# A second buffer for the split halves of v ahead of their DMA transpose

## The chip, the cores and the metric

The kernel runs on one core of a Trainium2 chip. The metric is the device time of one execution in microseconds (us), the median of several runs. The engines are TensorE (PE in the profile, with PEld for its weight loads), VectorE (DVE), ScalarE (ACT), GpSimd (POOL) and SyncE (SP), which here only issues DMAs. Each engine works through its own instructions in a fixed order; semaphores hold an instruction back until what it depends on is done.

## The reference

Causal attention with a bias from a running sum, for 8 batches of 8 heads, 576 positions and 64 channels, and then a feed-forward layer on its result:

```python
scores = scale * np.matmul(q, k.transpose(0, 1, 3, 2))
s_pos = np.maximum(s, 0.0)
cum = np.cumsum(s_pos, axis=-1)
bias = -(cum[:, :, :, None] - cum[:, :, None, :])
scores = np.where(causal, -1000000000.0, scores + np.minimum(bias, 0.0))
attn = softmax(scores)                       # with 1e-09 added to the sum
x = np.matmul(attn, v)                       # heads side by side: (4608, 512)
h = x @ w_in                                 # (4608, 2048)
g = np.where(h >= 1, h, np.where(h <= -1, 0.0, (h + 1) ** 2 / 4))
out = g @ w_out                              # (4608, 512)
```

All inputs and the output are float32.

## The kernel before

Most products are made of 16-bit parts: a float32 value is scaled and split into a high half and a low half (the remainder), and three of the four products of halves are summed. So `WI`, `WO`, `x`, `g`, `pb` and `vb` all have two halves.

**Jobs and slots.** The attention is cut into 64 jobs: for each batch, four pairs of heads for the first half of the positions (`hf` 0, positions 0 to 319) and then the same four pairs for the second half (`hf` 1). `att_slot(j, k)` traces slot k (0 to 7) of job j. Slot 0 prepares the operands of the scores (`att_prep`: `Q1s`, `K1s`, `Q2s`, `K2s`, lines 353 to 363), slot 1 of an `hf` 0 job prepares v (`v_prep`), slots 2 to 7 make the scores of one tile each, slot 5 of an `hf` 0 job turns v (`v_turn`), and slot 7 multiplies the weights of the job before with its v (`att_out`, line 474, into `px`). The feed-forward steps (`ffn_h`, line 528, and `ffn_y`, line 567) of an earlier half batch are traced between the slots. During the first two batches the weights `w_in` and `w_out` are also decoded and split on DVE, ACT and POOL.

**The way of v.** For each pair of heads n, counted through all batches (n = 4b + p), v lies in a float32 tile of 128 by 576 (`vraw`, loaded by line 256 on SP). `batch_v` (lines 260 to 265) works out the scales `rc` of a batch. `v_prep` opens the tile `vb` (128 by 2 by 640, float16): POOL zeroes its padding (line 371) and writes the high half, v times scale (line 372). For the first four tiles POOL makes the low half too (lines 374 and 375); for all others DVE does it in `v_turn` (line 382), queued behind a given step of the scores. Then line 384 has SP issue a DMA that transposes `vb` into `vt`, which `att_out` reads. `vt` has five buffers, `vb` one.

**The weights' way.** In `scores`, line 403 (POOL) zeroes an edge of the tile `p`, lines 408 to 412 (PE) make the scores `s`, line 417 (DVE) adds the mask and takes the minimum, line 428 (ACT) takes the exponential. `weights_t` then scales and splits the result into `pb`: `rs` (lines 444 and 445, DVE), high halves (lines 449 and 451, POOL), a scaling (line 450, ACT), low halves (line 452 POOL, line 455 DVE), and line 456 has SP issue the DMA transpose of `pb` into `pt`. In the feed-forward part, `u` comes from lines 540 to 544 (ACT, DVE), the high half of `g` from line 554 (ACT), the low half from line 555 (POOL).

**What sets the order.** The order of instructions on each engine isn't the order of the code. The program is built in a tile context with `schedule_with_timeline_sim=True`: when it is built, a simulated timeline runs along, and each engine is given, at each point of that timeline, an instruction whose inputs are ready and whose tile has a free buffer; among several the earlier in the code goes first, apart from blocks marked `high_priority` (a lead) and `issue_after` (behind a given instruction). A tile's buffer is free again when all its readers and writers are done: for `vb`, when the DMA transpose has landed. On the chip the order is fixed, and an instruction whose buffer isn't free yet holds up all that stands behind it on its engine.

Of the kernel before, what the change touches and what calls it, by code (L numbers as in the profile page):

```python
# [8 lines left out]
F16 = mybir.dt.float16  # L9
# [13 lines left out]
P = 128  # L23
# [4 lines left out]
SP = NB * P  # L28
# [45 lines left out]
def attention_ffn(ctx: ExitStack, tc: tile.TileContext, qT, kT, vT, s, w_in, w_out, yT):  # L74
# [5 lines left out]
    ap = ctx.enter_context(tc.tile_pool(name="ap", bufs=2))  # L80
# [284 lines left out]
    def v_prep(n):  # L365

        b, p = n // NPAIR, n % NPAIR
        v = vraw.pop((b, p))
        r = rcs[b][:, p:p + 1]
        VB = ap.tile([P, 2, SP], F16, tag="vb", bufs=1, name=f"vb{n}")  # L370
        G.memset(VB[:, :, S:], 0.0)
        G.tensor_scalar(VB[:, 0, :S], v, r, 1.0, ALU.mult, ALU.mult)
        if n < V_POOL:
            G.tensor_scalar(v, v, r, 1.0, ALU.mult, ALU.mult)
            G.tensor_tensor(VB[:, 1, :S], v, VB[:, 0, :S], ALU.subtract)
        vbs[n] = VB, v, r

    def v_turn(n):
        VB, v, r = vbs.pop(n)
        if n >= V_POOL:  # L380
            with tc.issue_after(ttr[0]):
                V.scalar_tensor_tensor(VB[:, 1, :S], v, r, VB[:, 0, :S], ALU.mult, ALU.subtract)
        VT = vts[n] = ap.tile([P, 2 * NB, P], F16, tag="vt", bufs=5, name=f"vt{n}")
        nc.sync.dma_start_transpose(out=VT, in_=VB.rearrange("p l n -> p (l n)"))
# [109 lines left out]
    def att_slot(j, k):  # L494

        if j < len(jobs):
            n, hf = jobs[j]
            if k == 0:
                att_prep(n, hf)
            if k == 1 and hf == 0:  # L500
                v_prep(n)
            if k == V_K and hf == 0:
                v_turn(n)
            if k >= 2:
                scores(n, *UNITS[hf][k - 2])
            if k == 3 and j + 1 < len(jobs):
                att_load(*jobs[j + 1])
            if k == 1 and j % (2 * NPAIR) == V_J and j // (2 * NPAIR) + 1 < B:
                load_v(j // (2 * NPAIR) + 1)
            if k == 5 and j + 1 < len(jobs) and jobs[j + 1][0] % NPAIR == 0 and jobs[j + 1][1] == 0:  # L510
                with tc.issue_after(ttr[0]):
                    batch_start(jobs[j + 1][0] // NPAIR)
        if k == OUT_K and 1 <= j <= len(jobs) and j != NPAIR:
            while j == len(jobs) and late:
                late.pop(0)()
            att_out(*jobs[j - 1])
# [171 lines left out]
```

## Time and profile before

| | us |
|---|---|
| median of 3 runs | 1111.91 |
| lowest and highest | 1111.22, 1112.82 |
| the profiled execution | 1112.3 |
| span of its instructions | 1110.2 |

The mean granted clock of TensorE over the span is 0.982 of full speed. The first 200 us are the start: weights are loaded, decoded and split there, and PE is far from full. From then on the slices of the span show PE at 9 tenths or more almost throughout. The page gives the busy time of each engine, 40 slices of the span, the DMA queues, the chain of work that ended last, and the costliest groups of instructions by line. The list of waits tells which engine stood still at which line, and what released it; the timeline has single instructions in order of time.

### The profile page before, as it was taken

Reading aid. Unit: us, or ns where it says so; the run is one execution under the profiler, and the core shown is the slowest. Engines: PE = TensorE matmul, PEld = TensorE weight load, DVE = VectorE, ACT = ScalarE, POOL = GpSimd, SP = SyncE. Lnnn points to the kernel's source line nnn. Section 1 sums busy time; section 2 is a strip of 40 time slices with the busy share of each in tenths; the row PEclk is TensorE's granted clock in tenths of the full one; section 3 lists DMA queues with packets and bytes.
Section 4 is the critical chain, followed back from the end, with each engine's and each line's share of the span. In section 5 each row is a group of like instructions: output and inputs, shape, how many; then the busy total and the mean of one; then the engine's idle time right before and its main releaser. Section 6 shows DMA issues by size and latency. Waiting matters only on the chain.

```text
span 1110.2 us, 25043 instructions
## 1 busy us (share of the span) xinstructions
PE 999.0 (90%) x8470; PEld 771.2 (69%) x8470; DVE 855.0 (77%) x2392; ACT 715.9 (64%) x1683; POOL 657.2 (59%) x1161
## 2 busy tenths in 40 slices
PE   0454799899999999999999999999999999899998
PEld 0132466588767877777777877787777877787787
DVE  7979987578868877878787877787777886887533
ACT  3647766467557775777567775877576755777432
POOL 3666275676647664766566755766476665765522
PEclk9997899699999999999999999999999999999999
DMA  8984536767638763987558763977387874666300
GB/s 257 241 174 129 186 78 126 140 120 152 127 84 187 165 151 72 181 164 158 106 119 186 156 149 74 193 155 167 68 178 155 170 129 80 152 156 138 68 24 20
DMA packets 339623, 153.70 MB, mean 138 GB/s; under 512 B 290728, under 2 KB 321320, under 8 KB 339496
## 3 DMA queue, kind: packets, MB, share of 16 engines
q1 hardware_dynamic: 329792, 142.17, 60.2%
q10 hardware_dynamic: 9704, 9.93, 2.9%
q8 instruction: 67, 1.10, 0.4%
q14 instruction: 60, 0.49, 0.1%
HBM read 71.00 MB, written 9.73 MB: 73 GB/s over the span
## 4 chain that ended last, share of the span: by engine, by line
PE 61%; DVE 15%; DMA 7%; POOL 7%; issue 6%; ACT 4%; ACTq 0%; DVEq 0%; SPq 0%; POOLq 0%
PE h L528 25%; PE y L567 24%; PE px L474 4%; DMA pt<-pb 4%; PE s L411 3%; DVE pb L455 3%; PE s L412 3%; DVE p L417 2%; POOL pb L449 2%; DVE Q1s L362 1%; ACT u L540 1%; PE s L408 1%; DMA wor<-in_moe_w_out_dram 1%; POOL pb L452 1%; DVE h L543 1%
## 5 line engine op out<-in xcount | busy, mean ns | idle before, releaser
L528 PE MATMUL h<-x,WI 128*128 128x256 f16 (+1 forms) x3072 | 463.5, 290 | 22.2 <-DVE u L544 19.6
L567 PE MATMUL y<-g,WO 128*128 128x256 f16 (+1 forms) x3072 | 453.0, 287 | 8.4 <-POOL g L555 6.5
L528 PEld LDWEIGHTS <-WI 128*128 128x128 f16 x3072 | 291.2, 99 | 116.3 <-issue 27.9
L567 PEld LDWEIGHTS <-WO 128*128 128x128 f16 x3072 | 288.1, 98 | 93.4 <-issue 13.8
L555 POOL TENSOR_TENSOR g<-u,g 128x320 f16<-128x320 f32 (+1 forms) x256 | 204.5, 799 | 161.2 <-ACT g L554 156.1
L428 ACT ACTIVATE p<-p,mn 64x64 f32<-64x64 f32 (+4 forms) x320 | 179.5, 561 | 140.2 <-DVE mn L417 123.0
L540 ACT ACTIVATE u<-h,ub,us 128x320 f32<-128x320 f32 (+1 forms) x256 | 149.3, 583 | 121.6 <-PE h L528 119.7
L543 DVE SCALAR_TENSOR_TENSOR h<-h,ws,u 128x320 f32<-128x320 f32 (+1 forms) x256 | 132.4, 517 | 96.9 <-ACT u L540 94.4
L449 POOL TENSOR_SCALAR pb<-p,rs 64x128 f16<-64x128 f32 (+4 forms) x160 | 95.3, 595 | 173.3 <-DVE rs L445 108.0
L452 POOL TENSOR_TENSOR pb<-p,pb 64x128 f16<-64x128 f32 (+4 forms) x160 | 169.1, 1057 | 9.3
L455 DVE SCALAR_TENSOR_TENSOR pb<-p,rs,pb 64x128 f16<-64x128 f32 (+4 forms) x160 | 132.3, 827 | 44.9 <-POOL pb L449 44.7
L417 DVE CUSTOM_DVE_ANT_0 p<-s,mask 64x64 f32<-64x64 f32 (+4 forms) x320 | 134.6, 421 | 33.5 <-PE s L412 17.4
L544 DVE SCALAR_TENSOR_TENSOR u<-u,r,h 128x320 f32<-128x320 f32 (+1 forms) x256 | 130.2, 509 | 6.2
L411 PE MATMUL s<-K1s,Q1s 128*128 128x288 f32 (+4 forms) x312 | 117.5, 378 | 11.4 <-DVE Q1s L362 7.1
L450 ACT ACTIVATE p<-p,rs 64x64 f32<-64x64 f32 (+4 forms) x160 | 89.5, 559 | 58.9 <-DVE rs L445 57.7
L554 ACT CAST g<-u 128x320 f16<-128x320 f32 (+1 forms) x256 | 108.1, 422 | 9.8 <-DVE u L544 9.1
L451 POOL TENSOR_SCALAR pb<-p 64x128 f16<-64x128 f32 (+4 forms) x160 | 93.9, 587 | 11.8 <-ACT p L450 10.0
L412 PE MATMUL s<-K2s,Q2s 68*128 68x288 f32 (+4 forms) x312 | 95.9, 307 | 1.1 <-DMA K2s<-cumd 0.7
L474 PEld LDWEIGHTS <-vt 128*64 128x64 f16 x1536 | 74.0, 115 | 32.9 <-issue 17.9
L474 PE MATMUL px<-pt,vt 128*64 128x256 f16 (+3 forms) x1536 | 84.1, 262 | 10.8 <-DMA pt<-pb 6.8
L411 PEld LDWEIGHTS s<-K1s,Q1s 128*128 128x128 f32 (+1 forms) x312 | 56.6, 181 | 21.2 <-issue 6.7
L363 DVE TENSOR_TENSOR K2s<-rk,K1s 64x1152 fp32r<-64x1152 f32 (+1 forms) x52 | 59.1, 1136 | 2.2 <-ACT K1s L360 0.9
(123 smaller groups left out, 963.3 us busy)
## 6 DMA issues: line engine op xcount, KB each, us to landing
rk<-in_k_dram SPq DMA_DIRECT2D x56, 288.0 KB
v<-in_v_dram SPq DMA_DIRECT2D x32, 288.0 KB
wir<-in_moe_w_in_dram SPq DMA_DIRECT2D x16, 512.0 KB
wor<-in_moe_w_out_dram SPq DMA_DIRECT2D x16, 512.0 KB
rk<-in_k_dram SPq DMA_DIRECT2D x48, 160.0 KB
rq<-in_q_dram SPq DMA_DIRECT2D x48, 160.0 KB
rq<-in_q_dram SPq DMA_DIRECT2D x56, 128.0 KB
out_dram<-o ACTq DMA_DIRECT2D x32, 160.0 KB
```

What stands on the lines that cost most here:

```text
L411: T.matmul(sc[:R, :c1 - c0], Q1[:, hd, qo:qo + R], K1[:, hd, c0:c1], start=True, stop=False)
L417: ttr[0] = V.tensor_tensor_reduce(out=Pt[:R, c0:c1], in0=sc[:R, :c1 - c0], in1=mask[:R, mo:mo + c1 - c0], scale=-0.125, scalar=3.0e38 if m ...
L428: A.activation(Pt[:R, :W], Pt[:R, :W], AF.Exp, bias=m2[:R], scale=-1.0, accum_out=sums[n, i][:R, hd:hd + 1])
L452: G.tensor_tensor(los[1], pw, his[1], ALU.subtract)
L455: V.scalar_tensor_tensor(los[0], pv, rs[:R, :1], his[0], ALU.mult, ALU.subtract)
L474: T.matmul(px[hd * D:(hd + 1) * D, lo:N], VT[:, vl * NB + j, hd * D:(hd + 1) * D], PT[:, 4 * j + 2 * hd + pl, lo:], start=(m == 0), stop=( ...
L528: T.matmul(h[:, :N], WI[4 * kt + ft // 4][:, wl, ft % 4 * P:(ft % 4 + 1) * P], x[:, kt, xl], start=(n == 0), stop=(n == 3 * NKT - 1),)
L540: first = A.activation(u, h[:, :N], AF.Relu, bias=ubi[b], scale=usc[b]).ins
L543: V.scalar_tensor_tensor(h[:, :N], h[:, :N], wsc[b], u, ALU.mult, ALU.max)
L544: V.scalar_tensor_tensor(u, u, r, h[:, :N], ALU.min, ALU.mult)
L555: G.tensor_tensor(g[:, 1], u, g[:, 0], ALU.subtract)
L567: T.matmul(ys[b, hf, m][:, :N], WO[8 * (m // 2) + ft // 2][:, wl, c0:c0 + P], g[:, gl], start=(ft == 0 and n == 0), stop=(ft == NFT - 1 an ...
```

## The change

The tile `vb` gets two buffers in place of one. Nothing else is edited; each buffer is 2560 bytes per partition.

```diff
-        VB = ap.tile([P, 2, SP], F16, tag="vb", bufs=1, name=f"vb{n}")
+        VB = ap.tile([P, 2, SP], F16, tag="vb", bufs=2, name=f"vb{n}")
         G.memset(VB[:, :, S:], 0.0)
         G.tensor_scalar(VB[:, 0, :S], v, r, 1.0, ALU.mult, ALU.mult)
```

With one buffer the memset of tile n + 1 depends on the transpose of tile n; with two, on that of tile n - 1.

## The prediction

> **What bounds the kernel now.** I read the page first, then the busy times by window, the list of waits, the timeline of one stall, and the instructions on the tile vb. From the page, the line on the engines:
>
> ```profile
> PE 999.0 (90%) x8470; PEld 771.2 (69%) x8470; DVE 855.0 (77%) x2392; ACT 715.9 (64%) x1683; POOL 657.2 (59%) x1161
> ```
>
> TensorE (PE) is busy for 999.0 of 1110.2 us, so the end is PE work plus PE's idle time. Once the start is over, each of the eight batches has a first stretch of some 40 us with the four jobs of the first half (`hf` 0, in which v is prepared), and a second one of some 84 us. The busy times by window (columns: window, its length, then busy time and instructions of each engine, granted clock, DMA share, GB/s) for the six later first stretches and one second stretch:
>
> ```profile
> 322.00:362.00 40.00, 35.81 (x343) 29.68 (x340) 30.68 (x97) 29.20 (x84) 26.88 (x62) 1.00 0.80 178
> ...
> 446.00:486.00 40.00, 35.47 (x340) 29.54 (x338) 30.48 (x95) 28.73 (x81) 26.45 (x61) 1.00 0.90 178
> 486.00:569.50 83.50, 83.50 (x722) 64.54 (x722) 67.56 (x185) 55.45 (x125) 49.60 (x81) 1.00 0.59 127
> 569.50:607.00 37.50, 35.14 (x339) 29.34 (x338) 30.31 (x94) 28.40 (x80) 26.45 (x60) 1.00 0.85 186
> ...
> 691.00:728.00 37.00, 35.11 (x339) 29.39 (x338) 29.82 (x94) 28.36 (x80) 26.56 (x61) 1.00 0.87 188
> ...
> 812.00:851.00 39.00, 35.19 (x339) 29.51 (x338) 30.32 (x94) 28.67 (x81) 26.32 (x60) 1.00 0.83 179
> ...
> 934.70:974.00 39.30, 35.07 (x339) 29.32 (x338) 30.50 (x94) 28.44 (x80) 26.97 (x60) 1.00 0.72 152
> ```
>
> In the second stretch PE has no idle time at all (83.50 of 83.50). In the six first stretches it idles for 4.19, 4.53, 2.36, 1.89, 3.81 and 4.23 us, 21.0 together. Nothing in the steady part of the kernel can give more than that. Who waits there, from the list of waits (engine, line, releaser: us in total, times, longest):
>
> ```profile
> DVE pb L455 <- POOL pb L449: 44.7, 52, 3.4
> POOL vb L371 <- DMA vt<-vb: 35.1, 24, 3.5
> ...
> PE s L411 <- DVE Q1s L362: 7.1, 7, 1.6
> ...
> PE y L567 <- POOL g L555: 6.5, 7, 1.3
> ...
> PE s L411 <- DVE mn L417: 3.8, 5, 1.0
> ```
>
> The second row is the wait that the change is about: the memset that opens the one vb buffer stands on POOL until the transpose of the tile before has landed, 35.1 us in 24 waits. One of them, from the timeline (start, duration, engine, line):
>
> ```profile
> 470.31 1.37 SPq L384 DMA_TRANSPOSE vt<-vb  x1
> ...
> 475.77 0.20 POOL L371 MEMSET vb<- 128x128 f16 x1 [3.49 <-DMA vt<-vb]
> ...
> 476.67 0.66 POOL L555 TENSOR_TENSOR g<-u,g 128x256 f16<-128x256 f32 x1
> ...
> 477.33 0.48 POOL L449 TENSOR_SCALAR pb<-p,rs 128x256 f16<-128x256 f32 x1
> 477.39 0.27 PE L567 MATMUL y<-g,WO 128*128 128x256 f16 x1 [1.14 <-POOL g L555]
> ...
> 477.85 0.61 DVE L455 SCALAR_TENSOR_TENSOR pb<-p,rs,pb 128x256 f16<-128x256 f32 x1 [3.37 <-POOL pb L449]
> ...
> 478.49 1.18 DVE L362 TENSOR_TENSOR Q1s<-rq,Q1s 64x640 fp32r<-64x640 f32 x1
> ...
> 479.81 0.21 PE L411 MATMUL s<-K1s,Q1s 128*64 128x64 f32 x1 [1.29 <-DVE Q1s L362]
> ```
>
> So the wait does reach PE: behind the memset are queued the scaling L372, g (L555) and L449; PE waits 1.14 us for g, and VectorE (DVE) 3.37 us for L449, which makes Q1s late and costs PE 1.29 us more. The question is whether a second buffer takes the wait away.
>
> **The change, part by part.** It removes no instruction and adds none: 32 memsets, 32 scalings, 32 transposes stay. It moves one condition: the memset of tile n+2, not of n+1, now waits for the transpose of tile n. Whether POOL still meets that wait depends on where the memset stands in POOL's order, which is fixed when the program is built, from a simulated timeline. How that order treats vb is seen from all instructions on the tile between 400 and 500 us, and then between 500 and 560 us (count: min/median/max ns, first and last start):
>
> ```profile
> L372 POOL TENSOR_SCALAR vb<-v,rc x4: 739/744/760, 427.3 to 476.0; 128x576 f16<-128x576 f32 x4
> L382 DVE SCALAR_TENSOR_TENSOR vb<-v,rc,vb x4: 802/850/1551, 446.1 to 485.2; 128x576 f16<-128x576 f32 x4
> L384 SPq DMA_TRANSPOSE vt<-vb x4: 1339/1365/1381, 448.7 to 486.1; - x4
> L371 POOL MEMSET vb<- x4: 204/204/209, 452.1 to 489.6; 128x128 f16 x4
> ```
>
> ```profile
> L372 POOL TENSOR_SCALAR vb<-v,rc x1: 746/746/746, 550.8 to 550.8; 128x576 f16<-128x576 f32 x1
> ```
>
> The last memset, at 489.6, stands 3.5 us behind the transpose issued at 486.1. It opens the tile of the next batch, whose scaling runs only at 550.8, 61 us later, when that batch's scales are there; in the code it belongs later still. In the same way the first scaling at 427.3 is 18.8 us ahead of its L382 at 446.1. So vb is not built where the code asks for it: the order puts the memset at the first place where a buffer is free by the simulated time, whether or not anybody needs it, and on the chip that place comes 1.5 us (35.1/24) too early. With two buffers the memset of n+2 is free at that very moment, the landing of transpose n, and its v and scales are there too. My reading: it takes the place that n+1 has now, with the same wait.
>
> What changes then, per batch: the first memset and scaling (4b+1) find their buffer free and move up beside those of 4b, into the second stretch. Behind transposes 4b and 4b+1 stand the pairs of 4b+2 and 4b+3, as now those of 4b+1 and 4b+2. Behind transpose 4b+2 stands only the memset of 4b+4, since the next batch's scales are missing; one scaling of 0.74 us leaves that place. Behind 4b+3 a lone memset stands as now.
>
> - The scaling that leaves: 0.74 us in each of seven batches, between 0 and 5.2 us. In the stall above it stood directly ahead of the g for which PE waited: -0.7 us. In the other batches the work behind it waits for something else anyway, as these rows of POOL's timeline show:
>
> ```profile
> 596.41 0.20 POOL L371 MEMSET vb<- 128x128 f16 x1 [1.56 <-PE s L412]
> ...
> 598.47 0.48 POOL L449 TENSOR_SCALAR pb<-p,rs 128x256 f16<-128x256 f32 x1 [0.48 <-DMA pt<-pb]
> ```
>
> L449 starts there when an earlier transpose of pb lands, with idle time to spare after the scaling, so 0 for them. I take -0.7, the value of the shown row.
> - The scaling that moves up: seven times 0.74 us of POOL in the second stretch. At its place the timeline of POOL has
>
> ```profile
> 427.32 0.74 POOL L372 TENSOR_SCALAR vb<-v,rc 128x576 f16<-128x576 f32 x1
> 428.91 0.79 POOL L555 TENSOR_TENSOR g<-u,g 128x320 f16<-128x320 f32 x1 [0.85 <-ACT g L554]
> 432.27 0.79 POOL L555 TENSOR_TENSOR g<-u,g 128x320 f16<-128x320 f32 x1 [2.57 <-ACT g L554]
> ```
>
> The 0.85 us of idle time ahead of the next g hide 0.74; without that cover it costs up to 0.74 x 7 = 5.2 us. I take 0. Were it to go below nothing, the gain would lie in the first bullet, since it is the same instruction.
> - The waits: from nothing changed to all 21.0 us of PE's idle time gone. I take 0, by the rows of 486.1, 489.6 and 550.8.
> - The start: tile 1 can be built right behind tile 0, in this idle time of POOL:
>
> ```profile
> 32.01 1.37 POOL L449 TENSOR_SCALAR pb<-p,rs 64x128 f16<-64x128 f32 x2 [4.84 <-DVE rs L444]
> ```
>
> but tile 2 then takes its place as above. In the first batch v is released by L375 on POOL, so the next batch's loads of v may also move up on SP's queue, into a stretch where DMA is full, by the windows and by the page's list of DMA issues:
>
> ```profile
> 23.00:50.00 27.00, 11.80 (x26) 5.29 (x26) 25.32 (x76) 16.06 (x37) 18.14 (x29) 1.00 0.98 251
> ```
>
> ```profile
> v<-in_v_dram SPq DMA_DIRECT2D x32, 288.0 KB
> ```
>
> Each of them takes 288 KB / 251 GB/s = 1.15 us there, ahead of the weights that are loaded behind it. So the start lies between a gain of 4.84 us and a loss of 4.6, four loads; I take 0, since one tile takes the other's place.
>
> The sum against the profiled execution's own time: 1112.3 - 0.7 = 1111.6 us (span 1110.2 and 2.1 around it). The profile ran 0.4 us above the median of the runs, 1111.9, so the forecast of a median is 1111.9 - 0.7 = 1111.2.
>
> **The rivals.** *The wait goes.* If the memset and scaling of n+2 are put later than transpose n's landing, POOL runs on, and g and L449 come 1.5 us earlier. The waits of PE for Q1s (7.1 us) mostly stay, since L449 then waits for pb's transposes as in the row of 598.47; the rest of the idle time, 21.0 - 7.1 = 13.9 us, goes: 1111.9 - 13.9 = 1098.0. For it speaks that a memset which nobody needs for long can stand later: the lone one of 489.6 waited less than the mean of 1.5 us,
>
> ```profile
> 489.61 0.20 POOL L371 MEMSET vb<- 128x128 f16 x1 [0.26 <-DMA vt<-vb]
> ```
>
> and with two buffers all are of that kind. Against it: an early place is taken whenever POOL is idle, and POOL is idle for a third of a first stretch (26.45 busy of 40). If half of the 13.9 us goes, the time is 1105.
>
> The Trainium skill (Perfetto Trace Analysis, Optimization Strategy) says that the same gap repeating on an engine that ought to be saturated can mean too few buffers for the next tile. By that rule this rival would hold; the trace agrees that the gap repeats, but not that more buffers move the memset away from the landing.
>
> *Slower: the early scaling lands in front of g.* From the second bullet: if the scaling of 4b+1 takes longer than the 0.85 us that cover it, g is late in a stretch where PE has no slack. All executions of the scaling in the run:
>
> ```profile
> L372 POOL TENSOR_SCALAR vb<-v,rc x32: 738/746/1401, 23.6 to 963.6; 128x576 f16<-128x576 f32 x32
> ```
>
> It decides from 0.85 us, and the longest took 1.40. Seven batches at 0.74 give 1111.2 + 5.2 = 1116.4. Against it: the next place on POOL, ahead of the g at 432.27, has 2.57 us of cover.
>
> The Trainium skill (SBUF — State Buffer, SBUF: two separate sides) states that GpSimd and certain VectorE operations hold a shared port pair as an exclusive lock, the other standing still. By that rule a moved scaling could take or cause such a stretch; the spread of 738 to 1401 ns agrees with it, but no row here shows the lock itself.
>
> *The change does nothing:* every memset keeps its place and so does every scaling: 1111.9.
>
> **How the numbers follow.** The wait stays, with at most one scaling gained: 0.50, 1111.2, own range 1108.5 to 1113.5, for the order of other instructions may shift a little. The wait goes wholly or in part: 0.27, 1098.0 to 1107. Slower: 0.18, 1114 to 1118. Nothing at all: 0.05. A difference under 0.2% (2.2 us) can't be told from no change in this kernel. Faster by more: the 0.27 and 0.09 of the first case, 0.36. Within: 0.42. Slower: 0.18 and 0.04 of the first, 0.22. The range reaches from 1100, leaving out the lower third of the second case (0.09), to 1117 (0.05 left out above).
>
> **What would show it.** Right: in the trace after, L371 still waits for the transpose some 25 times for about 35 us, at the same places, each now for the tile after next (each L382 a whole job further behind its L372), and PE's idle time in the first stretches is still near 20 us. The rival of the gain is right if that wait is under 10 us and the first stretches come to 36 to 37 us. The slower one is right if a second stretch has PE idle in front of L567, released by POOL's g, shortly after a second L372. The forecast is wrong if the new order changes the first 200 us: PE is far from full there, and a few us either way would show in the end at once.

## The result and the profile after

The change makes the kernel slower: 1120.42 us, median of four runs (1119.52 to 1121.40), against 1112.37 (1111.22 to 1114.62) for the kernel before in the same session. The ratio is 1.0070, with a 95% interval of 1.0051 to 1.0089, so the cost is 5.7 to 9.9 us. The forecast was 1111.2, with a range of 1100 to 1117; the time lies outside it.

The line on the engines, from the page of the kernel after, whose span is 1117.4 us:

```profile
PE 998.8 (89%) x8470; PEld 771.3 (69%) x8470; DVE 862.6 (77%) x2392; ACT 716.0 (64%) x1683; POOL 657.7 (59%) x1161
```

PE works as long as before (999.0 us); the 7.2 us by which the span grew are idle time of PE. From the list of waits of the kernel after (us in total, times, longest):

```profile
POOL vb L371 <- DMA vt<-vb: 41.3, 27, 4.6
...
PE s L411 <- DVE Q1s L362: 7.0, 7, 1.6
PE y L567 <- POOL g L555: 6.9, 8, 1.0
```

The wait that the change was about is still there, and longer: 41.3 us in 27 waits where it was 35.1 in 24. PE's two waits behind it are what they were (7.1 and 6.5 before). All instructions on vb between 400 and 500 us show where the memsets stand (count: min/median/max ns, first and last start):

```profile
L372 POOL TENSOR_SCALAR vb<-v,rc x4: 745/746/798, 433.3 to 468.9; 128x576 f16<-128x576 f32 x4
...
L384 SPq DMA_TRANSPOSE vt<-vb x4: 1360/1380/1705, 454.6 to 492.5; - x4
L371 POOL MEMSET vb<- x4: 204/204/209, 458.1 to 496.1; 128x128 f16 x4
```

The last memset, at 496.1, again stands 3.6 us behind the transpose issued at 492.5. The places on POOL are the old ones; each is now taken by the tile after the one that had it. So these places give the steady part no reason to win or to lose. The place of the loss is seen in one instruction for each batch, the last step of its scales (line 265). First the kernel before, in two stretches (185 to 310 us and 910 to 925 us), then the kernel after in the matching ones:

```profile
L265 DVE TENSOR_SCALAR rc<-rc x2: 170/171/172, 190.0 to 304.3; 128x4 f32<-128x4 f32 x2
...
L265 DVE TENSOR_SCALAR rc<-rc x1: 676/676/676, 915.2 to 915.2; 128x4 f32<-128x4 f32 x1
```

```profile
L265 DVE TENSOR_SCALAR rc<-rc x2: 170/170/170, 195.2 to 310.4; 128x4 f32<-128x4 f32 x2
...
L265 DVE TENSOR_SCALAR rc<-rc x1: 675/675/675, 922.9 to 922.9; 128x4 f32<-128x4 f32 x1
```

The kernel after is 5.2 us late at 190 us, 6.1 at 304 and 7.7 at 915. Most of the loss is there before the steady part begins. The start's busy times from 20 to 60 us (columns as in the prediction), of the kernel before and of the one after:

```profile
20.00:60.00 40.00, 16.19 (x53) 8.59 (x54) 37.78 (x117) 24.41 (x55) 24.33 (x41) 1.00 0.97 238
```

```profile
20.00:60.00 40.00, 14.47 (x49) 7.13 (x49) 38.45 (x106) 21.42 (x48) 26.88 (x43) 1.00 0.91 211
```

POOL does 2.55 us more in these 40 us, and what the decoding of the weights needs is less: 27 GB/s less is moved, 1.08 MB in all, or 4.5 us at the rate of before, and ACT, which begins the decoding of each weight tile, does 3.0 us less. SP's queue shows where the loads went. The kernel before:

```profile
27.20 1.52 SPq L384 DMA_TRANSPOSE vt<-vb  x1
30.28 1.00 SPq L192 DMA_DIRECT2D wir<-in_moe_w_in_dram  x2
...
35.95 1.19 SPq L456 DMA_TRANSPOSE pt<-pb  x1
37.31 0.47 SPq L192 DMA_DIRECT2D wir<-in_moe_w_in_dram  x1
```

and the kernel after:

```profile
28.85 1.44 SPq L384 DMA_TRANSPOSE vt<-vb  x1
30.40 0.65 SPq L192 DMA_DIRECT2D wir<-in_moe_w_in_dram  x1
31.14 1.44 SPq L384 DMA_TRANSPOSE vt<-vb  x1
36.16 1.17 SPq L456 DMA_TRANSPOSE pt<-pb  x1
...
40.23 3.83 SPq L192 DMA_DIRECT2D wir<-in_moe_w_in_dram  x4
```

Before, two weight loads stood behind the first transpose, at 30.28. After, tile 1 is built straight behind tile 0, its transpose and those of `pb` stand ahead of the eleventh weight load, and four loads come together at 40.23. Two more things are new: POOL stands still for the lone memset of tile 4,

```profile
53.37 0.20 POOL L371 MEMSET vb<- 128x128 f16 x1 [4.62 <-DMA vt<-vb]
```

and at 200 us the matmuls of line 474 wait 4.14 us for a `pt` where they waited 2.46. The kernel before,

```profile
203.51 2.77 PE L474 MATMUL px<-pt,vt 128*64 128x256 f16 x30 [2.46 <-DMA pt<-pb]
```

and the kernel after:

```profile
195.42 1.47 POOL L372 TENSOR_SCALAR vb<-v,rc 128x576 f16<-128x576 f32 x2 [2.88 <-DVE rc L265]
...
203.93 1.27 SPq L384 DMA_TRANSPOSE vt<-vb  x1
205.29 6.07 SPq L456 DMA_TRANSPOSE pt<-pb  x3
...
211.14 2.77 PE L474 MATMUL px<-pt,vt 128*64 128x256 f16 x30 [4.14 <-DMA pt<-pb]
```

Two scalings run together there (tiles 4 and 5), and on SP the transpose of v now goes ahead of those of `pb`. Which of these makes the loss is a question for the experiments.

### The profile page after: what moved, and what is told of

It reads as the page before. It is cut to its first block, busy times and chain, and to the rows that moved or that the text cites. A ratio compares the mean times of both kernels' runs of the same rounds, so it can differ in the third digit from the quotient of the medians.

```text
span 1117.4 us, 25045 instructions
## 1 busy us (share of the span) xinstructions
PE 998.8 (89%) x8470; PEld 771.3 (69%) x8470; DVE 862.6 (77%) x2392; ACT 716.0 (64%) x1683; POOL 657.7 (59%) x1161
## 4 chain that ended last, share of the span: by engine, by line
PE 59%; DVE 15%; DMA 9%; POOL 7%; issue 6%; ACT 4%; ACTq 0%; SPq 0%; DVEq 0%; POOLq 0%
PE h L528 24%; PE y L567 24%; PE px L474 5%; DMA pt<-pb 4%; PE s L411 3%; DVE pb L455 3%; PE s L412 3%; DMA wir<-in_moe_w_in_dram 2%; DVE p L417 2%; POOL pb L449 2%; POOL pb L452 2%; ACT u L540 2%; DMA wor<-in_moe_w_out_dram 2%; DVE h L543 1%; ACT p L428 1%
## 5 line engine op out<-in xcount | busy, mean ns | idle before, releaser
L455 DVE SCALAR_TENSOR_TENSOR pb<-p,rs,pb 64x128 f16<-64x128 f32 (+4 forms) x160 | 136.5, 853 | 45.8 <-POOL pb L449 45.5
```

Source lines behind the costliest of these rows:

```text
L455: V.scalar_tensor_tensor(los[0], pv, rs[:R, :1], his[0], ALU.mult, ALU.subtract)
```

## The experiments

The edit is of one kind throughout. `weights_t` keeps its instructions of lines 451 and 452 as marks, and the memset and the scaling of a tile n are queued on POOL behind a chosen mark. They can't be placed earlier than that; the planner still decides how much later. Nothing is left out of the computation.

```diff
+    marks, behind = {}, lambda n: ...
     def v_prep(n):
+        hold = lambda at: tc.issue_after(marks[at[:2]][at[2]]) if at else ExitStack()
...
-        G.memset(VB[:, :, S:], 0.0)
-        G.tensor_scalar(VB[:, 0, :S], v, r, 1.0, ALU.mult, ALU.mult)
+        with hold(behind(n)): G.memset(VB[:, :, S:], 0.0)
+        with hold(behind(n)): G.tensor_scalar(VB[:, 0, :S], v, r, 1.0, ALU.mult, ALU.mult)
...
-        G.tensor_scalar(his[1], pw, 1.0, 1.0, ALU.mult, ALU.mult)
-        G.tensor_tensor(los[1], pw, his[1], ALU.subtract)
+        mark = G.tensor_scalar(his[1], pw, 1.0, 1.0, ALU.mult, ALU.mult).ins
+        marks[n, i] = mark, G.tensor_tensor(los[1], pw, his[1], ALU.subtract).ins
```

`behind(n)` gives (tile whose job it is, score tile, 0 for line 451 or 1 for line 452), or nothing, which leaves the tile free. Below only `behind` is shown. Ratios are to the kernel before on the same chip, with 95% intervals; its medians there were 1113.4 to 1114.7 us.

**The start put back, two buffers.** Theory A: the whole loss is the order of the start. Theory B: it is the second buffer itself, or its steady part.

```diff
+    behind = lambda n: {1: (0, 0, 0), 2: (0, 2, 0), 3: (1, 2, 1), 4: (3, 0, 1), 5: (4, 2, 1)}.get(n)
```

> Two buffers, but the memset and scaling of tiles 1 to 5 are queued behind the same POOL instructions as in the kernel before; later tiles are free. Theory A (the 8 us come from the changed order of the first 210 us, and the steady part is unchanged because each memset only takes the place of the one before): 1110 to 1114 us, as before, with L371 still waiting some 25 times for 33 to 40 us. Theory B (the second buffer itself costs: its addresses, or the moved scalings in the later batches): stays at 1118 to 1121.

Measured: 1.0002 [0.9989, 1.0016]. DVE, ACT and SP then have exactly the order of before. POOL has it too up to the start's end; behind it one scaling of each batch stands earlier, as the prediction had it. The wait is the old one to the tenth, and PE's behind it are nearly so (7.1 and 6.5 before; list of waits):

```profile
POOL vb L371 <- DMA vt<-vb: 35.1, 25, 3.2
...
PE s L411 <- DVE Q1s L362: 7.4, 7, 1.6
...
PE y L567 <- POOL g L555: 5.6, 7, 1.2
```

So theory A holds: the places of five tiles in the start make the whole loss, and behind them a second buffer alone is worth nothing that could be measured.

**Which part of the start.** Five runs put some of these five tiles back and leave the others free.

```diff
+    behind = lambda n: {4: (3, 0, 1), 5: (4, 2, 1)}.get(n)                    # tiles 4 and 5
+    behind = lambda n: {1: (0, 0, 0), 2: (0, 2, 0), 3: (1, 2, 1)}.get(n)      # tiles 1 to 3
+    behind = lambda n: {5: (4, 2, 1)}.get(n)                                  # tile 5
+    behind = lambda n: {1: (0, 0, 0)}.get(n)                                  # tile 1
+    behind = lambda n: {2: (0, 2, 0), 3: (1, 2, 1)}.get(n)                    # tiles 2 and 3
```

> Two buffers, order of the start as in the changed kernel, except that the memsets of tiles 4 and 5 and the scaling of tile 5 are queued on POOL where the kernel before has them (behind L452 of the fourth and the fifth job). PE, DVE, ACT and SP keep the changed kernel's order. Theory P (the stall of POOL does it): the 4.6 us for which the memset of tile 4 waits at 49 to 53 us, and the scaling of tile 5 ahead of L449 at 195 us, are the loss. Then the ratio to the kernel before falls to 0.998 to 1.002. Theory W (the order of tiles 1 to 3 does it, since the weight loads on SP's queue and the decoding behind them come in another order): the ratio stays at 1.005 to 1.009, and the third L224 starts 4 us or more later than in the kernel before (166.6 us).

> Two buffers; tiles 1 to 3 are queued where the kernel before has them, tiles 4 and 5 stand where the planner puts them. Theory W (order of tiles 1 to 3): ratio to the kernel before 0.998 to 1.002, the second L224 starts by 138 us (136.4 before, 141.0 in the changed kernel). Theory P (POOL held up by the early memsets and scalings of tiles 4 and 5): the ratio stays at 1.005 to 1.009. If each has a part, it lies between, at 1.002 to 1.005.

> As the changed kernel, except that the memset and the scaling of tile 5 are queued on POOL where the kernel before has them, so that only one scaling stands ahead of L449 at 195 us. If the pair makes the late pb and with it the wait of 4.14 us of PE for pt at 204 to 211 us (2.46 before), 1.5 to 3 us come back: ratio 1.004 to 1.006. If the loss is older (the 4.6 us by which the second L224 is late at 136 us are simply carried on), the ratio stays at 1.006 to 1.009.

> As the changed kernel, except that tile 1 alone is queued on POOL where the kernel before has it. On SP's queue the eleventh and the twelfth of the first weight loads (L192) then stand ahead of the transposes of the first job again, as before; the later ones, the loads of v and the tiles 2 to 5 keep a changed order. Theory S (the loss is that SP's queue holds weight loads behind transposes that wait for POOL: 204 GB/s between 20 and 40 us in the changed kernel against 245 before, four loads at 40.2 us at once): the rate in that window is back over 235 GB/s, and more than half of the loss goes, ratio 1.000 to 1.004. Theory R (the rest of the new order does it, with or without the early tile 1): the rate may come back, and the ratio stays at 1.005 to 1.009.

> The counterpart of the run with tile 1 alone in its old place (1.0078 [1.0055, 1.0102]): here tile 1 stands where the planner puts it, straight behind tile 0, and tiles 2 and 3 are queued where the kernel before has them; tiles 4 and 5 are free. On SP's queue the weight loads from the eleventh on then stand behind the first job's transposes as in the changed kernel, while three of the four loads of the next batch's v have their old places among them. If tiles 2 and 3 in front of POOL's score work are the loss, the third L224 starts by 168 us as in the kernels that were not slow (165.3 to 167.4) and the ratio comes to 1.001 to 1.005. If any early tile is enough to upset the order of the decoding, the third L224 starts at 171 us or later (171.6 to 172.6 in the slow ones) and the ratio is 1.005 to 1.009.

Measured, with the rate from 20 to 60 us, the start of the third line 224 (the end of the scales for the second half of `w_out`), and DVE's busy and idle time up to that start, each from one trace:

| tiles in their old places | ratio | GB/s, 20 to 60 us | third L224, us | DVE busy, idle until then, us |
|---|---|---|---|---|
| all (kernel before) | 1 | 238 | 166.6 | 141.5, 25.1 |
| 1 to 5 | 1.0002 [0.9989, 1.0016] | 239 | 166.7 | 140.6, 26.1 |
| 1 to 3 | 1.0027 [1.0014, 1.0040] | 236 | 167.1 | 144.1, 23.0 |
| 2 and 3 | 1.0055 [1.0041, 1.0070] | 210 | 170.7 | 143.6, 27.1 |
| 1 | 1.0078 [1.0055, 1.0102] | 212 | 172.6 | 147.7, 24.9 |
| 4 and 5 | 1.0076 [1.0061, 1.0091] | 214 | 172.5 | 146.9, 25.6 |
| 5 | 1.0082 [1.0062, 1.0102] | 214 | 171.6 | 145.2, 26.4 |
| none (the change) | 1.0070 [1.0051, 1.0089] | 211 | 171.7 | 147.8, 23.9 |

Rows of three of them, first tiles 1 to 3 in their old places, then tile 1 alone, then tiles 2 and 3 (the window, and all executions of line 224 on `r_wo`):

```profile
20.00:60.00 40.00, 17.37 (x55) 9.22 (x56) 36.75 (x116) 24.69 (x56) 25.89 (x46) 1.00 0.98 236
...
L224 DVE TENSOR_SCALAR r_wo<-r_wo x2: 139/146/154, 138.6 to 167.1; 128x1 f32<-128x1 f32 x2
```

```profile
20.00:60.00 40.00, 15.62 (x52) 8.51 (x52) 38.95 (x110) 22.75 (x50) 27.02 (x45) 1.00 0.87 212
...
L224 DVE TENSOR_SCALAR r_wo<-r_wo x2: 148/151/154, 143.2 to 172.6; 128x1 f32<-128x1 f32 x2
```

```profile
20.00:60.00 40.00, 16.91 (x54) 9.15 (x55) 33.30 (x109) 22.06 (x54) 27.07 (x44) 1.00 0.89 210
...
L224 DVE TENSOR_SCALAR r_wo<-r_wo x2: 146/150/154, 141.1 to 170.7; 128x1 f32<-128x1 f32 x2
```

The stall of POOL for tile 4 (4.62 us in the kernel after) is not the loss: with tiles 4 and 5 held back that wait is gone and the time is not better. Nor is the pair of scalings at 195 us: tile 5 held back gives nothing. Tiles 1 to 3 decide, and only together: with all three in place the ratio falls to 1.0027, with tile 1 alone nothing is won, with 2 and 3 at most little. What is left at 1.0027 would belong to tiles 4 and 5 and shows only once the others are right; its interval just overlaps that of the first run. My expectation for tile 1 alone was right about the rate between 20 and 40 us (265 GB/s) and wrong about what follows from it: the stretch from 40 to 60 us then fell to 160, so that the missing bytes had only moved. The rows with and without the loss separate cleanly on rate and start: where any of tiles 1 to 3 stands early, some 25 GB/s are missing between 20 and 60 us, and the third line 224 comes 4 to 6 us late.

That the missing loads make it late does not follow, and the traces give little for it. ACT's waits for weight loads between 20 and 60 us come to 6.1 us in the kernel after and to 7.0 in the kernel before; behind 60 us its waits for those of `w_out` grow from 9.0 to 16.1, but DVE, which does most of the decoding, was not held up longer. Its busy time up to the third line 224 (the third figure behind the comma), before and after:

```profile
0.00:166.60 166.60, 87.40 (x470) 52.60 (x471) 141.54 (x383) 100.79 (x194) 91.65 (x143) 0.94 0.67 178
```

```profile
0.00:171.70 171.70, 89.32 (x468) 53.79 (x469) 147.79 (x382) 101.52 (x195) 91.14 (x144) 0.94 0.66 172
```

For about as many instructions DVE is busy 6.2 us longer, and idle 1.2 us less: what it does takes longer. In the last column this holds for most of the delay in the four rows in which tiles 2 and 3 stand early; in the row of tiles 2 and 3 half of the delay is idle time. The longest of these instructions is one of the decoding, in the kernel before, in the kernel after and with tile 1 alone in place:

```profile
37.37 2.49 DVE L208 SCALAR_TENSOR_TENSOR WO<-wir,WO 128x512 int32<-128x512 int32 x1
```

```profile
37.59 4.16 DVE L208 SCALAR_TENSOR_TENSOR WO<-wir,WO 128x512 int32<-128x512 int32 x1
```

```profile
37.04 4.49 DVE L208 SCALAR_TENSOR_TENSOR WO<-wir,WO 128x512 int32<-128x512 int32 x1
```

The same step takes 0.68 us at 30.45 in the kernel after. At 37.59 POOL works there without a pause, mostly on tiles 1 and 2, until 41.20, and DVE's instruction ends at 41.75:

```profile
39.13 1.27 POOL L375 TENSOR_TENSOR vb<-v,vb 128x576 f16<-128x576 f32 x1
...
40.46 0.74 POOL L374 TENSOR_SCALAR v<-v,rc 128x576 f32<-128x576 f32 x1
43.24 0.89 POOL L449 TENSOR_SCALAR pb<-p,rs 128x384 f16<-128x384 f32 x1 [2.04 <-ACT p L428]
```

In the kernel before POOL's last step on tile 1 ends at 39.31 and DVE's instruction at 39.86, as far behind it:

```profile
38.04 1.27 POOL L375 TENSOR_TENSOR vb<-v,vb 128x576 f16<-128x576 f32 x1
```

In both kernels DVE's instruction lasts until POOL's run of work is over, and the moved tile makes that run longer. This one instruction is not the whole loss: the scales of `w_in` (line 224 on `r_wi`) are ready at 81.8 us, 1.0 us late, and the first of `w_out` at 141.0, 4.6 us late, so most of the delay arises between the two. How it divides among drawn-out instructions, DVE's new order and the loads is open: no run changed the order of one engine alone.

**Is the wait worth anything?** The rival of the gain was tried next: from tile 5 or 6 on, memset and scaling are queued late, behind line 452 of a third score tile. With one buffer, with two, and with two and the start left free:

```diff
+    behind = lambda n: (n - 1, 2, 1) if n > 4 and n % NPAIR else None    # one buffer
+    behind = lambda n: {...}.get(n) if n < 6 else (n - 2, 2, 1)          # two, start as in the first run
+    behind = lambda n: (n - 2, 2, 1) if n > 5 else None                  # two, start free
```

> One buffer as before; from tile 5 on, the memset and scaling of a tile that isn't the first of its batch are queued behind L452 of the last tile of scores of the job before, some 4 us later than now. If the stalls of POOL at the memset cost PE its idle time (theory A): 1098 to 1106 us, the wait at L371 under 10 us, PE idle in the first stretches 7 to 12 us instead of 21. If PE's idle time belongs to the transposes of pb anyway: within 0.3% of 1112. If the scaling is now late for L382: 1114 to 1120, with a new wait of DVE L382 for POOL L372.

> Two buffers, the start as in the kernel before (tiles 1 to 5 queued as there), and from tile 6 on memset and scaling queued behind L452 of the last tile of scores two jobs back, when the transpose has long landed and the scaling is not urgent. Theory A: 1096 to 1102 us, the wait at L371 under 5 us. If PE's idle time belongs to pb's transposes: 1108 to 1113.

> As the run with the late memsets and two buffers, but the start is left as in the changed kernel. Theory A (start and steady part add): 6 to 8 us above that run, 1103 to 1110 us. Theory B: the same as that run.

Measured: 0.9974 [0.9960, 0.9988], 0.9980 [0.9966, 0.9993] and 1.0072 [1.0049, 1.0096]. The gain of 6 us and more that the first two were to show, if the wait made PE's idle time, did not come. The third against the second shows the start's cost once more, 0.9% (10.3 us where 6 to 8 were expected). The second is the instructive one. The wait for the transpose is gone from its list, and yet it wins no more than the kernel with one buffer, which still waits 14.1 us. From its page, and from its list of waits:

```profile
PE 1007.0 (91%) x8470; PEld 776.6 (70%) x8470; DVE 858.7 (77%) x2392; ACT 718.5 (65%) x1683; POOL 663.3 (60%) x1161
```

```profile
PE s L412 <- DMA K2s<-cumd: 6.9, 3, 2.6
```

Its span is 1110.2 us, as before, so PE's idle time fell from 111.2 to 103.2 us while PE's busy time rose by 8.0. The windows around one of the three new waits (the third figure from the end is the granted clock) and the wait itself show what else is new:

```profile
690.00:697.00 7.00, 5.32 (x60) 4.25 (x58) 4.78 (x15) 4.96 (x12) 3.63 (x10) 1.00 0.92 179
697.00:700.30 3.30, 1.91 (x14) 1.51 (x15) 1.92 (x9) 0.98 (x5) 2.29 (x6) 1.00 1.02 208
700.30:703.70 3.40, 3.15 (x13) 1.88 (x12) 3.40 (x12) 2.63 (x10) 2.44 (x7) 0.51 1.15 210
```

```profile
698.13 0.21 PE L412 MATMUL s<-K2s,Q2s 68*64 68x64 f32 x1 [2.64 <-DMA K2s<-cumd]
```

Holding back only by the job two ahead changes the order of all engines, a score matmul now comes before its operand, and the clock is halved behind the gap. Four such spells of this profile, at 454.6, 700.3, 823.2 and 946.1 us, last 20.4 us together; the last of them follows a wait of 1.31 us for ACT. The mean granted clock of all twelve runs of this kernel is 0.971 to 0.976, against 0.981 to 0.986 with one buffer.

**One buffer against two, late in the same way.** The last edit takes the anchor of the one-buffer kernel for the second to fourth tile of a batch and uses the second buffer only for the first tile, which nobody needs for 60 us:

```diff
+    behind = lambda n: {...}.get(n) if n < 6 else (n - 1, 2, 1) if n % NPAIR else (n - 2, 2, 1)
```

> Two buffers, start queued as in the kernel before; from tile 6 on the memset and the scaling of a tile are queued behind L452 of the third score tile of the job ahead of it (of the job two ahead for the first tile of a batch). DVE and SP then keep the order of the one-buffer kernel that does the same (0.9974 [0.996, 0.9988]); only the memsets of each batch's first tile move on POOL. If POOL's wait at L371 is all that counts, 14.1 us of wait in that kernel go to under 3 and the ratio comes to 0.994 to 0.997. If what is left to PE is no longer released by this wait (Q1s, pt, the clock after gaps), the ratio is that of the one-buffer kernel, 0.996 to 0.999, and the second buffer is worth nothing here either.

Measured: 0.9911 [0.9890, 0.9931], better than expected. Since its profile was ahead already where both kernels have the same order, both were run again side by side.

> The same program as the two-buffer kernel with late memsets and scalings (0.9911 [0.989, 0.9931]), beside the one-buffer one on the same chip. Its profile was 3.9 us ahead of the one-buffer kernel's at 220 us already, in a stretch where both have the same order, and 11.1 us at the end. If the second buffer is worth the 7 us that came after 220 us, this kernel is 0.4 to 0.8% faster than the one-buffer one; if the first profile and its runs were lucky in the start, under 0.3%.

> The same program as the one-buffer kernel with late memsets and scalings (0.9974 [0.996, 0.9988]). It should come to 0.996 to 0.999 again; the difference to the two-buffer kernel of this call, on one chip, is what the second buffer is worth once the order uses it.

Measured: two buffers 1105.40 us, 0.9923 [0.9905, 0.9941]; one buffer 1110.01 us, 0.9971 [0.9954, 0.9988]. The intervals don't overlap: here the second buffer is worth 4.6 us of the 8.2. The waits of PE from 222 to 1105 us in the one-buffer kernel, and one row of its whole list:

```profile
PE s L411 <- DVE Q1s L362: 7.7, 7, 1.4
...
PE y L567 <- POOL g L555: 1.8, 4, 0.8
```

```profile
POOL vb L371 <- DMA vt<-vb: 14.5, 7, 3.1
```

and in the two-buffer kernel, where that last row is gone:

```profile
PE s L411 <- DVE Q1s L362: 5.4, 6, 1.3
PE y L567 <- ACT g L554: 2.3, 8, 0.4
...
PE y L567 <- POOL g L555: 0.5, 2, 0.3
```

The seven waits that one buffer leaves are those of the lone memset, once for each batch. The second buffer lets this memset go ahead of the transpose, and PE's two waits fall by 2.3 and 1.3 us. That is 3.6 us between two profiles whose spans differ by 2.7 (1107.2 and 1104.5); the 4.6 are between medians, so how much of them is these waits isn't settled.

## Why the prediction failed

**The steady part was read rightly.** It said that the wait would stay, the memset of tile n + 2 taking the place of tile n + 1. It stayed (41.3 us in 27 waits, 4.62 of them in the start), and with the old start it is 35.1 us in 25. The scaling that leaves its place was put at -0.7 us; with 1.0002 [0.9989, 1.0016] a gain of that size can't be told from none. The scaling that moves up was put at nothing, with up to 5.2 us if g came late: PE's wait for POOL's g went from 6.5 to 6.9 us, and in the second stretch from 490 to 575 us of the kernel after PE is busy for 85.00 of 85.00, so the slower rival by this path did not occur.

**The start is the step that failed.** The prediction put it at 0, between -4.84 and +4.6 us, "since one tile takes the other's place". Measured, it is the whole loss, 5.7 to 9.9 us. Three things were wrong. The argument is that of the steady part, where a place is passed on because nothing else is ready; in the start tiles 1 to 3 all have their v and their scales as soon as tile 0 has them, so every free buffer moves a tile forward in earnest. The upper bound counted only the loads of v, four at 1.15 us, as what a moved tile triggers. These did not move up at all: the kernel before issues the first of them at 42.77 us, the kernel after all four from 69.19 on.

```profile
69.19 1.99 SPq L256 DMA_DIRECT2D v<-in_v_dram  x4
```

What moved was the tile's other work: its steps on POOL, beside which an instruction of the decoding on DVE took 4.16 us in place of 2.49, its own transpose (line 384) and with it those of `pb`, on the same queue of SP as the weight loads; 1.08 MB less came in between 20 and 60 us. And the prediction counted POOL's idle time there as free to fill and put no price on what runs beside it, though up to the third line 224 DVE is busy for 141.5 of 166.6 us in the kernel before, and for 6.2 us more in the kernel after. It named such a drawn-out stretch beside its slower rival, for the steady part alone. Which of these paths carries how much of the loss stays open. The sentence that a new order of the first 200 us would break the forecast named the risk and gave it little weight: beside the slower rival of the steady part, the chances left 0.04.

**The rival of the gain** did not come by itself, for the reason given against it. The sentence beside it, on the Trainium skill (Perfetto Trace Analysis, Optimization Strategy), said that by its rule this rival would hold; the measurement decides against that for this change, where the same gap became 41.3 us. Forced by the order, the gain is real but smaller than the 13.9 us priced: 8.2 us on the median (1113.56 to 1105.40). The price let the 7.1 us of waits for Q1s stand and all other idle time of PE go. In the two-buffer kernel 5.4 us of the waits for Q1s are left, and some 6 us of others, 2.3 of them for ACT's g.

## What to carry to other kernels

Where a planner puts work at the first free place, a further buffer does not remove a wait, it moves work forward; ask for every stage what will stand earlier on each queue, its DMAs included, and what runs beside it, above all in the start, where most inputs are ready at once. To find out whether a buffer or an order is at fault, give the new buffer the old order: one run settled it here. A buffer becomes worth its place when the order uses it, here 4.6 us with the memset queued late enough.

## What was not expected of the hardware

In the first two-buffer kernel with late memsets, waits of PE of 1.31 to 2.64 us were followed by a halved granted clock: the gap that ended at 698.13 was followed by 3.4 us at 0.51 from 700.3 on, with PE busy for 1.91 of the 3.30 us between. PE was busy for 0.82 to 2.34 of the 3.4 us ahead of each of the four spells. By an estimate from these rows, 20.4 us at half the clock cost at most 10.2 us of work at full clock; PE's busy time is 8.0 us above that of the kernel before. How much of the 8.0 is the spells' isn't settled, since the one-buffer kernel with late memsets, without such a spell behind 216 us, has 1001.9 us where the kernel before has 999.0. The Trainium skill (TensorE: Matmul & The Clock Gate, HAM oscillation — how this bites in real kernels) gives as a rule that PE should have no idle gaps above about 3.4 us. The trace doesn't bear it out as the limit: 2.64 us and less, with loose work around it, did it here. Nor did every gap do it: in the run with the old start, PE waited seven times for Q1s, up to 1.6 us, and the clock stayed at full speed from 216 us to the end of the span.
